# Who transposes the rows of experts 0 and 1: TensorE in place of VectorE

## The chip, the cores and the metric

The kernel runs on one core of a Trainium2 chip. Its engines are TensorE (PE: matrix products, with PEld for its weight loads), VectorE (DVE), ScalarE (ACT), GpSimd (POOL) and SyncE (SP), which here issues the DMA transfers. The metric is the device time of one execution in microseconds. Before the change three runs took 1133.36, 1134.56 and 1135.92 us, with a median of 1134.56.

## The reference

Three layers follow one another on 2304 tokens of width 512 (4 batches x 576 positions, 8 heads of 64):

```
scores = q k^T / 8 + decay (sums of log f), causal softmax, times v       -> x (2304 x 512)
h = x w_in (512 x 2048);  x = (h * sigmoid(1.702 h)) w_out (2048 x 512)
logits = x w_gate + log1p(exp(x w_noise)) * noise;  the two best of 8 experts, softmax of the two
out = sum over both of  weight * (max(x w1[e], 0) w2[e])                  (w1: 512 x 1024, w2: 1024 x 512)
```

The result is float32. The kernel gets that precision on TensorE by splitting each operand in a rounded part (hi) and a remainder (lo) and adding three products: hi x hi, lo x hi, hi x lo.

## The kernel before, in words

The order of all instructions is written at build time by a planner (class `Planner`, line 57). Every piece of work is a generator that yields operations with an engine and an estimated time, waits for events, or takes numbered tokens (a buffer). When several operations are ready on an engine, the one with the lowest priority number goes first. Each engine then runs its list in order, SyncE's list of transfers too; on the chip an instruction still waits until its inputs are there and its buffer is free.

The first expert layer (w_in, w_out) runs over 9 chunks of 256 tokens, in four passes over quarters of the hidden width. In its last pass each finished chunk is routed (`route`, line 1143): TensorE transposes the 2 x 4 blocks of the chunk (line 1159), ScalarE copies the rounded part (1162), VectorE subtracts the remainder (1163), then come the logits, some 25 small VectorE operations that find the two experts and the places, and four indirect writes by GpSimd (line 1264) that put each token's row, 512 values and 4 of metadata (`ROW` = 516), into the table `tab` at the place of its expert. Priority numbers of this layer start at 10000.

The second layer works on groups of table rows (`group`, line 1374). There are ten: group 0 and 1 hold the first 256 rows of experts 0 and 1 and are loaded early, when the sixth of nine chunks has been scattered; groups 2 and 3 hold their other 384 rows; groups 4 to 9 hold 640 rows each of experts 2 to 7. Group g has priority 20000 + 100 g; the transposes of its rows have 130 less, its weights 30 less. A group's rows are loaded by SyncE (line 1402), transposed (1435), copied by ScalarE (1438), subtracted by VectorE (1439); then for each of 8 blocks of the hidden width comes the first product h (line 1496), the copies of its parts (1479, 1480), and the second product ye (1549), whose result is scaled and added to the output by an indirect transfer (1536).

VectorE's transpose works on 32 x 32 squares only. So the rows are loaded with four transfers for each part, one for each 32 partitions, each row in four pieces of 128 values (512 bytes), such that the squares that VectorE transposes lie right:

```
for i in range(4):
    nc.sync.dma_start(t[32 * i:32 * i + 32, 4 * b0_:4 * b1_], bass.AP(
        tensor=tab.tensor, offset=tab.offset + (r0 + b0_ * 128) * ROW + i * part,
        ap=[[ROW, 32], [32 * ROW, 4 * (b1_ - b0_)], [1, part]]))
```

The columns of w_out are permuted on the host so that the features of a row come out in the order that this needs, and w1 is used as it is. The 4 values of metadata come with one more transfer for each group (line 1407).

Weights (`wprep`, line 348) are loaded in blocks of 256 KB into one of four staging buffers (`stok`, `NST` = 4), rounded by ScalarE (398), subtracted by VectorE or GpSimd (345, 346), and kept in 5 places for w1 and 6 for w2. The four staging buffers also serve the routing, which takes two of them for its transposed parts until the logits are done, and groups 0 and 1: each takes two, one for the rows as loaded (`xe`) and one for the rows as transposed (`xf`), and later one for each scaled output block. Groups 2 to 9 have buffers of their own.

Of the kernel before, what the change touches and what calls it, by code (L numbers as in the profile page):

```python
# [17 lines left out]
DRAM = bass.MemoryType.DRAM  # L18

TINY = 2.0 ** -15  # L20
CAP = 640
EARLY = 256
NEE = 2
ROW = 516
# [182 lines left out]
def dma(nbytes):  # L207
    return 0.05 + nbytes / RATE
# [7 lines left out]
def tile_attn_mlp_moe(ctx, tc, q, k, v, f, w_in, w_out, gates, noise, w1, w2, out):  # L216
# [52 lines left out]
    def c_(shape, name, dt=F32):  # L269
        return const.tile(shape, dt, name=name)  # L270
# [1098 lines left out]
    eids = [c_([128, NBE], f"eids{e}", I32) for e in EE]  # L1369
    ewab = [c_([128, 2, NBE], f"ewab{e}") for e in EE]  # L1370
    xftok = Tokens(range(2))
    emeta = [c_([128, NBE, ROW - DM], f"emeta{e}") for e in EE]

    def group(gi_):
        e, b0, b1 = groups[gi_]
        nb = b1 - b0
        N = nb * 128
        small = gi_ < len(EE)
        prio = 20000 + gi_ * 100
        if small:  # L1380
            yield scat[FLOOR]
            xs_, fs = yield from stages(2)
            t = stage(xs_, [128, 4 * nb, DM // 4], F32, "xe")
            xf = stage(fs, [128, nb, KD, 128], F32, "xf")
            ids, wab, mt = eids[gi_], ewab[gi_], emeta[gi_]
        else:
            yield m2_go
            xs_ = yield xetok
            xf = None
            t = M["x"].tile([128, 4 * nb, DM // 4], F32, name="xe", tag=f"xe{xs_}")  # L1390
            mt = M["x"].tile([128, nb, ROW - DM], F32, name="mt", tag=f"mt{gi_}")
            ids = M["x"].tile([128, nb], I32, name="ids", tag=f"ids{gi_}")
            wab = M["x"].tile([128, 2, nb], F32, name="wab", tag=f"wab{gi_}")
        r0 = e * RS + b0 * 128
        part = DM // 4
        parts = [(0, nb)] if gi_ <= 2 else [(0, 2), (2, nb)]
        lev = [event() for _ in parts]
        mev = event()

        def load(b0_, b1_):  # L1400
            for i in range(4):
                nc.sync.dma_start(t[32 * i:32 * i + 32, 4 * b0_:4 * b1_], bass.AP(
                    tensor=tab.tensor, offset=tab.offset + (r0 + b0_ * 128) * ROW + i * part,
                    ap=[[ROW, 32], [32 * ROW, 4 * (b1_ - b0_)], [1, part]]))

        def meta():
            nc.sync.dma_start(mt, tab[r0:r0 + N, DM:ROW].rearrange("(b p) c -> p b c", p=128))
        for (b0_, b1_), z in zip(parts, lev):
            yield ("go", one_op(("DMA", dma((b1_ - b0_) * 128 * DM * 4), lambda b0_=b0_, b1_=b1_: load(b0_, b1_), 4), z))
        yield ("go", one_op(("DMA", 0.4, meta), mev))  # L1410
        if small:
            for z in lev:
                yield z
            yield mev
            loads[0] -= 1
            if not loads[0]:
                yield ("set", early_ok)
            sl = yield ring
            x = xslot(sl)
            hi_, lo_ = x.hi, x.lo  # L1420
        else:
            sl = yield xttok
            hi_, lo_ = [M["x"].tile([128, KD, N], FR, name=f"xt{z}", tag=f"xt{z}{sl}") for z in "hl"]
        stt = nc.vector.scalar_tensor_tensor
        tev = [event() for _ in range(nb)]

        def xtr(b, z):
            yield z
            hi, lo = hi_[:, :, b * 128:(b + 1) * 128], lo_[:, :, b * 128:(b + 1) * 128]
            if small:  # L1430
                raw = xf[:, b]
            else:
                fi = yield xftok
                raw = M["x"].tile([128, KD, 128], F32, name="xf", tag=f"xf{fi}")
            yield ("DVE", dve(512), lambda: nc.vector.transpose(
                raw.rearrange("p k (j b) -> p j k b", b=32),
                t[:, 4 * b:4 * b + 4].rearrange("p j (k a) -> p j k a", a=32)))
            yield ("ACT", act(512, True), lambda: nc.scalar.copy(hi, raw))
            yield ("DVE", dve(512), lambda: nc.vector.tensor_tensor(lo, raw, hi.bitcast(F32), op=OP.subtract))
            if not small:  # L1440
                yield (xftok, fi)
            yield ("set", tev[b])
        for (b0_, b1_), z in zip(parts, lev):
            for b in range(b0_, b1_):
                yield ("go", xtr(b, z), prio - XTP)
        yield mev
        yield V(lambda: stt(wab[:, 0], mt[:, :, 3], float(NT), block[:, 0:nb], op0=OP.is_ge, op1=OP.mult))
        yield V(lambda: nc.vector.tensor_tensor(ids, mt[:, :, 3], wab[:, 0], op=OP.add))
        yield V(lambda: stt(wab[:, 0], mt[:, :, 2], float(e), mt[:, :, 0], op0=OP.is_equal, op1=OP.mult))
        yield V(lambda: stt(wab[:, 1], mt[:, :, 2], float(e), mt[:, :, 1], op0=OP.not_equal, op1=OP.mult))  # L1450
        yield V(lambda: nc.vector.tensor_tensor(wab[:, 0], wab[:, 0], wab[:, 1], op=OP.add))
        for z in tev:
            yield z
        yield (stok if small else xetok, xs_)
        if small:
            yield (stok, fs)

        if gi_:
            yield mm1_end[gi_ - 1]
        halves = [(0, N)] if N <= 512 else [(0, N // 2), (N // 2, N)]  # L1460
        H_ = []
        hev = [event() for _ in range(FB)]
        yield ("go", second(gi_, H_, hev, ids, wab, prio), prio - 5)
        for j in range(FB):
            wt = W2[gi_, "a", j]
            yield wt.ready
            if small:
                hs = yield gtok
                hh, hl = [gplace[hs].tile([128, N], FR, name=f"g{z}", tag=f"g{z}{hs}") for z in "hl"]
            else:  # L1470
                hs = yield htok
                hh, hl = [M["h"].tile([128, N], FR, name=f"h{z}", tag=f"h{z}{hs}") for z in "hl"]
            H_.append((hh, hl, hs))
            a0, a1 = [z.rearrange("p (k n) -> p k n", k=KD) for z in (wt.hi, wt.lo)]
            ops = [(a, z, kk) for a, z in ((a0, hi_), (a0, lo_), (a1, hi_)) for kk in range(KD)]
            ends = []

            def evac(ps, hh, hl, c0, c1, bi, end):
                yield ("ACT", act(c1 - c0), lambda: nc.scalar.activation(hh[:, c0:c1], ps, AF.Relu))  # L1479
                yield ("DVE", dve(c1 - c0), lambda: stt(  # L1480
                    hl[:, c0:c1], ps, 0.0, hh[:, c0:c1].bitcast(F32), op0=OP.max, op1=OP.subtract))
                yield (banks, bi)
                yield ("set", end)

            def both(ends, end):
                for z in ends:
                    yield z
                yield ("set", end)
            for c0, c1 in halves:
                bi = yield banks  # L1490
                ps = bank(bi, "h")[:, :c1 - c0]

                def part(i0, i1):
                    for i in range(i0, i1):
                        a, z, kk = ops[i]
                        nc.tensor.matmul(ps, a[:, kk], z[:, kk, c0:c1], start=(i == 0), stop=(i == len(ops) - 1))  # L1496
                yield ("PE", mm(c1 - c0, 6), lambda: part(0, 6))
                yield ("PE", mm(c1 - c0, 6), lambda: part(6, 12))
                end = event()
                ends.append(end)  # L1500
                yield ("go", evac(ps, hh, hl, c0, c1, bi, end), prio - 20)
            yield ("go", both(ends, hev[j]))
            yield from wt.used()
        if small:
            yield (ring, sl)
        else:
            yield (xttok, sl)
        yield ("set", mm1_end[gi_])
# [89 lines left out]
    with tc.If(most > 0), ExitStack() as octx:  # L1598
# [3 lines left out]
        for e in range(E):  # L1602
# [13 lines left out]
            with tc.For_i(0, nb) as i:  # L1616
# [10 lines left out]
                                               op0=OP.not_equal, op1=OP.mult)  # L1627
                nc.vector.tensor_tensor(wa, t1, t2, op=OP.add)
                nat = one.tile([128, KD, 4, 32], F32, name="nat")
                nc.vector.tensor_copy(nat, row[:, 0:DM].rearrange("p (i k a) -> p k i a", i=4, k=KD))  # L1630
                ps = psum.tile([128, KD, 128], F32, name="otr")
                for kk in range(KD):
                    nc.tensor.transpose(ps[:, kk], nat[:, kk].rearrange("p i a -> p (i a)"), identf)
# [19 lines left out]
def lay(I):  # L1653
# [16 lines left out]
    def words(w):  # L1670
# [6 lines left out]
    gates = gates.reshape(-1, 128, gates.shape[1]).transpose(1, 0, 2)  # L1677
    noise = I["moe2_noise"]
    noise = noise.reshape(-1, 128, noise.shape[1]).transpose(1, 0, 2)
    a = dict(q=q, k=k, v=v, f=I["f"], w_in=words(blocks(I["moe_w_in"])), w_out=words(I["moe_w_out"][:, order]), gates=gates,  # L1680
             noise=noise, w1=blocks(I["moe2_w1"]), w2=I["moe2_w2"])
    return {n: np.ascontiguousarray(x) for n, x in a.items()}


# [16 lines left out]
```

## Time and profile before

| | |
|---|---|
| median of three runs | 1134.56 us |
| profiled execution | 1138.96 us, span 1137.1 us, mean granted clock 0.989 |
| TensorE matmul | 1092.4 us busy, 96% of the span |
| VectorE / ScalarE / GpSimd | 716.3 / 516.8 / 248.1 us, 63% / 45% / 22% |
| DMA | 168.85 MB, 148 GB/s over the span |
| chain that ended last | PE 73%, DVE 9%, DMA 4%, issue 3% |

Times are from the span's start. Attention, with the first products of the first expert layer between its work, runs until 233 us; that layer ends at about 644 us, the second layer's last matmul at about 1118 us; the last output transfers and the closing test for overfull experts follow. "Granted clock" is the share of 2.4 GHz that TensorE was given: 1.00 or about 0.5 (1.2 GHz) in a short stretch.

### The profile page before, as it was taken

To read this page: it belongs to the slowest core of one execution; us is meant where nothing else is said; L and a number is where in the kernel's file an instruction comes from. 1 tells how busy PE (TensorE), PEld (TensorE's weight loads), DVE (VectorE), ACT (ScalarE), POOL (GpSimd) and SP (SyncE) were. 2 spreads that over 40 slices of the span, in tenths; PEclk is the share of its full clock that TensorE was granted. 3 is DMA by queue.
4 is the path that set the end of the run, shared out by engine and by line. 5 is a ranking of instruction groups with operands and counts; after the bars stand their busy time and mean duration, and the time that the engine had idled before them with its cause. 6 is when DMAs were issued, how large, how long until landed. Compare 5 with 4: busy or idle time off the path is not lost.

```text
span 1137.1 us, 18945 instructions
## 1 busy us (share of the span) xinstructions
PE 1092.4 (96%) x6836; PEld 960.6 (84%) x6836; DVE 716.3 (63%) x1783; ACT 516.8 (45%) x1234; POOL 248.1 (22%) x283
## 2 busy tenths in 40 slices
PE   9999989999999999999999998899999999999993
PEld 7778768898998998998999876789999999999992
DVE  7899988856688459446888887476353535353310
ACT  6688777745453334224333444355233334242311
POOL 2245423321012001001244340132030303030302
PEclk9999999999999999999999999999999999999997
DMA  7767666767869913000112478987353635252403
GB/s 228 235 224 245 190 216 200 183 182 185 279 169 313 378 38 105 10 1 10 39 75 79 146 231 215 219 211 187 98 127 115 131 117 116 88 113 85 103 1 50
DMA packets 111897, 168.85 MB, mean 148 GB/s; under 512 B 16752, under 2 KB 54384, under 8 KB 111792
## 3 DMA queue, kind: packets, MB, share of 16 engines
q1 hardware_dynamic: 103152, 147.53, 43.6%
q0 software_dynamic: 8640, 20.00, 8.5%
q8 instruction: 56, 0.92, 0.4%
q14 instruction: 49, 0.40, 0.1%
HBM read 118.16 MB, written 49.32 MB: 147 GB/s over the span
## 4 chain that ended last, share of the span: by engine, by line
PE 73%; DVE 9%; DMA 4%; issue 3%; ACT 2%; POOL 1%; SPq 0%; POOLq 0%; ACTq 0%; DVEq 0%
PE h L951 17%; PE h L1496 17%; PE ye L1549 16%; PE y L971 16%; PE O L745 3%; DMA wraw<-in_w 2%; DVE pt24l L457 1%; PE PT L699 1%; ACT e L591 1%; PE S L610 1%; DVE e L585 1%; DVE wbl L345 1%; DMA out<-yt,eids 1%; PE tr L1159 1%; POOL out L1536 1%
## 5 line engine op out<-in xcount | busy, mean ns | idle before, releaser
L1480 DVE SCALAR_TENSOR_TENSOR hl<-h,hh 128x320 fp32r<-128x320 f32 (+1 forms) x112 | 55.7, 498 | 187.3 <-ACT hh L1479 187.2
L1479 ACT ACTIVATE hh<-h 128x320 fp32r<-128x320 f32 (+1 forms) x112 | 49.8, 445 | 215.9 <-PE h L1496 215.7
L1536 POOL DMA_INDIRECT out<-yt,ids x36 | 61.0, 1693 | 281.6 <-ACT yt L1531 274.2
L1549 PE MATMUL ye<-wbh,hh 128*128 128x512 f32 x288 | 114.4, 397 | 1.0 <-ACT hh L1479 1.0
L1549 PE MATMUL ye<-wbh,hl 128*128 128x512 f32 x288 | 114.7, 398 | 0.1
L1549 PE MATMUL ye<-wbl,hh 128*128 128x512 f32 x288 | 114.5, 397 | 0.0
L971 PE MATMUL y<-wbh,gh 128*128 128x512 f32 x288 | 113.4, 394 | 0.6 <-DVE pt01l L457 0.3
L971 PE MATMUL y<-wbh,gl 128*128 128x512 f32 x288 | 112.9, 392 | 0.3 <-POOL gl L346 0.2
L971 PE MATMUL y<-wbl,gh 128*128 128x512 f32 x288 | 112.7, 391 | 0.0
L926 ACT ACTIVATE t<-h 128x256 f32<-128x256 f32 x144 | 55.3, 384 | 121.8 <-PE h L951 109.7
L591 ACT ACTIVATE e<-e,m 128x128 f32<-128x128 f32 (+2 forms) x144 | 83.1, 581 | 29.7 <-DVE m L585 29.1
L1496 PE MATMUL h<-xth,wah 128*128 128x320 f32 (+1 forms) x448 | 85.7, 313 | 3.2 <-ACT wah L398 3.2
L927 DVE SCALAR_TENSOR_TENSOR t<-t,h 128x256 f32<-128x256 f32 x144 | 60.2, 418 | 43.0 <-ACT t L926 37.0
L1496 PE MATMUL h<-xtl,wah 128*128 128x320 f32 (+1 forms) x448 | 87.0, 313 | 0.0
L1496 PE MATMUL h<-xth,wal 128*128 128x320 f32 (+1 forms) x448 | 85.7, 313 | 0.0
L346 POOL TENSOR_TENSOR gl<-t,gh 128x256 fp32r<-128x256 f32 x28 | 29.6, 1059 | 237.5 <-PE h L951 191.2
L1496 PEld LDWEIGHTS h<-xth,wah 128*128 128x128 f32 x448 | 73.2, 188 | 8.3 <-ACT wah L398 3.5
L929 ACT CAST gh<-t 128x256 fp32r<-128x256 f32 x125 | 50.7, 406 | 55.1 <-DVE t L927 55.0
L1496 PEld LDWEIGHTS h<-xtl,wah 128*128 128x128 f32 x448 | 72.3, 188 | 0.8
L1496 PEld LDWEIGHTS h<-xth,wal 128*128 128x128 f32 x448 | 71.6, 188 | 0.0
L345 DVE TENSOR_TENSOR gl<-t,gh 128x256 fp32r<-128x256 f32 x116 | 50.8, 439 | 29.0 <-ACT gh L929 26.9
L345 DVE TENSOR_TENSOR wbl<-wraw,wbh 128x512 fp32r<-128x512 f32 x76 | 57.1, 753 | 18.8 <-ACT wbh L398 17.9
(417 smaller groups left out, 2627.3 us busy)
## 6 DMA issues: line engine op xcount, KB each, us to landing
wraw<-in_w SPq DMA_DIRECT2D x160, 256.0 KB
tab<-padr SPq DMA_DIRECT2D x40, 258.0 KB
x<-xo SPq DMA_DIRECT2D x32, 288.0 KB
bb<-cneg SPq DMA_DIRECT2D x15, 576.0 KB
wraw<-in_w_in SPq DMA_DIRECT2D x16, 512.0 KB
wraw<-in_w_out SPq DMA_DIRECT2D x16, 512.0 KB
out<-padr SPq DMA_DIRECT2D x23, 256.0 KB
xa<-x SPq DMA_DIRECT2D x22, 256.0 KB
```

Of the source, the lines that this page charges most:

```text
L345: return ways(kind, ("DVE", dve(n), lambda: nc.vector.tensor_tensor(dst, a, b, op=OP.subtract)), ("POOL", pool2(n), lambda: nc.gpsimd.tens ...
L591: yield ("ACT", act(n, True, extra=2), lambda: nc.scalar.activation(dst, dst, AF.Exp, bias=m[:, x:x + 1], scale=-1.0, accum_out=sa[:, shar ...
L926: yield ("ACT", act(CH), lambda: nc.scalar.activation(t, h, AF.Tanh, scale=0.851))
L927: yield ("DVE", dve(CH), lambda: nc.vector.scalar_tensor_tensor(t, t, 1.0, h, op0=OP.add, op1=OP.mult))
L929: yield ways("gh", ("ACT", act(CH, True), lambda: nc.scalar.copy(gh, t)), ("POOL", pool1(CH), lambda: nc.gpsimd.tensor_tensor(gh, t, onec. ...
L951: nc.tensor.matmul(h, a[:, kk], z[:, kk], start=(i == 0), stop=(i == len(ops) - 1))
L971: nc.tensor.matmul(y, a[:, t * 128:(t + 1) * 128], b, start=(fl == 0 and n == 0), stop=(fl == FPQ - 1 and n == 2))
L1479: yield ("ACT", act(c1 - c0), lambda: nc.scalar.activation(hh[:, c0:c1], ps, AF.Relu))
L1480: yield ("DVE", dve(c1 - c0), lambda: stt(hl[:, c0:c1], ps, 0.0, hh[:, c0:c1].bitcast(F32), op0=OP.max, op1=OP.subtract))
L1496: nc.tensor.matmul(ps, a[:, kk], z[:, kk, c0:c1], start=(i == 0), stop=(i == len(ops) - 1))
L1536: st = nc.gpsimd.indirect_dma_start(out=out, out_offset=bass.IndirectOffsetOnAxis(ap=ids[:, b:b + 1], axis=0), in_=yt, in_offset=None, com ...
L1549: nc.tensor.matmul(ye[b][0], a[:, b * 128:(b + 1) * 128], w, start=(j == 0 and n == 0), stop=(j == FB - 1 and n == 2))
```

## The change

`PEX` = 2 names the experts, 0 and 1, whose groups (0 to 3) are now "whole". Their rows are loaded as they lie in the table, 2064 bytes a row with the metadata, one transfer for each block of 128 rows. TensorE transposes each block with four 128 x 128 transposes into a PSUM bank, from which ScalarE copies and VectorE subtracts. The rows of w1 of these two experts are permuted on the host in the same way as the columns of w_out. The buffers for transposed rows and for early metadata are gone for groups 0 and 1, so each takes one staging buffer. Groups 4 to 9 keep VectorE's transpose; the planner's price for their loads is doubled, that for their metadata raised from 0.4 to 1.0. The branch for overfull experts, which doesn't run work here, follows the layout.

```diff
+PEX = 2
-    emeta = [c_([128, NBE, ROW - DM], f"emeta{e}") for e in EE]
+        whole = e < PEX
         if small:
             yield scat[FLOOR]
-            xs_, fs = yield from stages(2)
-            t = stage(xs_, [128, 4 * nb, DM // 4], F32, "xe")
-            xf = stage(fs, [128, nb, KD, 128], F32, "xf")
-            ids, wab, mt = eids[gi_], ewab[gi_], emeta[gi_]
+            xs_ = yield stok
+            t = stage(xs_, [128, nb, ROW], F32, "xe")
+            ids, wab = eids[gi_], ewab[gi_]
...
-        parts = [(0, nb)] if gi_ <= 2 else [(0, 2), (2, nb)]
+        parts = [(b, b + 1) for b in range(nb)] if whole else [(0, 2), (2, nb)]
         def load(b0_, b1_):
+            if whole:
+                nc.sync.dma_start(t[:, b0_], tab[r0 + b0_ * 128:r0 + b1_ * 128, :])
+                return
...
-            yield ("go", one_op(("DMA", dma((b1_ - b0_) * 128 * DM * 4), lambda b0_=b0_, b1_=b1_: load(b0_, b1_), 4), z))
-        yield ("go", one_op(("DMA", 0.4, meta), mev))
+            yield ("go", one_op(
+                ("DMA", dma((b1_ - b0_) * 128 * DM * (4 if whole else 8)), lambda b0_=b0_, b1_=b1_: load(b0_, b1_),
+                 1 if whole else 4), z))
+        if whole:
+            mt = t[:, :, DM:ROW]
+        else:
+            yield ("go", one_op(("DMA", 1.0, meta), mev))
...
-            if small:
-                raw = xf[:, b]
+            if whole:
+                bi = yield banks
+                raw = bank(bi, "tr").rearrange("p (k n) -> p k n", k=KD)
+
+                def go():
+                    for kk in range(KD):
+                        nc.tensor.transpose(raw[:, kk], t[:, b, kk * 128:(kk + 1) * 128], identf)
+                yield ("PE", TR * KD, go)
             else:
...
-            yield ("ACT", act(512, True), lambda: nc.scalar.copy(hi, raw))
+            yield ("ACT", act(512, not whole), lambda: nc.scalar.copy(hi, raw))
             yield ("DVE", dve(512), lambda: nc.vector.tensor_tensor(lo, raw, hi.bitcast(F32), op=OP.subtract))
-            if not small:
-                yield (xftok, fi)
+            yield (banks, bi) if whole else (xftok, fi)
...
+    w1 = np.concatenate([I["moe2_w1"][:PEX][:, order], I["moe2_w1"][PEX:]])
-             noise=noise, w1=blocks(I["moe2_w1"]), w2=I["moe2_w2"])
+             noise=noise, w1=blocks(w1), w2=I["moe2_w2"])
```

## Rows read from the trace of the kernel before

**Rows 1.** Stretches: busy PE, PEld, DVE, ACT, POOL; PE clock, DMA share, GB/s.

```profile
600.00:640.00 40.00, 39.99 (x274) 36.18 (x273) 34.26 (x160) 14.00 (x36) 13.94 (x25) 1.00 0.29 94
640.00:670.00 30.00, 27.07 (x175) 22.46 (x174) 25.91 (x118) 13.86 (x31) 10.00 (x16) 1.00 0.55 176
...
680.00:700.00 20.00, 16.55 (x86) 12.84 (x85) 11.64 (x23) 8.02 (x17) 2.64 (x3) 0.91 0.93 221
700.00:710.00 10.00, 9.60 (x50) 7.64 (x50) 9.14 (x21) 6.01 (x12) 0.00 (x0) 1.00 0.67 196
710.00:730.00 20.00, 16.83 (x77) 14.75 (x76) 8.04 (x19) 6.72 (x14) 3.27 (x3) 0.91 1.04 242
...
750.00:770.00 20.00, 18.84 (x89) 15.39 (x88) 15.03 (x24) 9.35 (x18) 6.10 (x6) 1.00 1.01 237
770.00:1113.00 343.00, 343.00 (x1908) 310.35 (x1906) 145.98 (x273) 115.66 (x236) 56.82 (x63) 1.00 0.42 104
```

**Rows 2.** The same table for two short stretches behind gaps of PE.

```profile
688.70:691.90 3.20, 3.20 (x9) 2.53 (x9) 1.91 (x6) 0.62 (x1) 0.00 (x0) 0.51 1.18 259
722.60:726.00 3.40, 3.40 (x10) 2.64 (x9) 1.99 (x3) 1.57 (x3) 0.00 (x0) 0.51 1.18 245
```

**Rows 3.** Waits of PE, 620 to 800: us in total, times, longest.

```profile
PE h L1496 <- ACT wah L398: 3.5, 2, 3.2
PE ye L1549 <- ACT gh L1479: 3.4, 3, 2.4
PE l L1189 <- DVE lgs L1182: 1.3, 1, 1.3
```

**Rows 4.** Timeline of SyncE's queue, 625 to 700: start, us, line, transfer, count.

```profile
630.33 1.82 SPq L1402 DMA_DIRECT2D xe<-tab  x4
...
641.95 45.19 SPq L365 DMA_DIRECT2D wraw<-in_w  x23
```

**Rows 5.** Chain that ended last, 600 to 800: start, us, what.

```profile
604.86 1.43 PE h L951 x12
606.41 0.93 PE tr L1159 x8
...
710.62 7.21 DMA out<-yt,eids
...
720.51 0.63 ACT wah L398
...
769.50 4.18 PE ye L1549 x18
```

**Rows 6.** Waits of SyncE's queue, 600 to 800: us in total, times, longest.

```profile
SPq L365 <- DMA out<-yt,eids: 12.1, 4, 6.2
...
SPq L365 <- DVE ewab L1447: 4.9, 1, 4.9
```

**Rows 7.** Timelines of DVE and PE: start, us, engine, line, operation, [idle].

```profile
632.89 0.68 DVE L1323 SCALAR_TENSOR_TENSOR pay<-y,yacc 128x512 f32<-128x512 f32 x1
...
643.82 1.03 PE L1159 MATMUL tr<-identf,pay 128*128 128x128 f32 x8
...
693.47 1.31 DVE L1435 STREAM_TRANSPOSE xf<-xe 128x512 f32<-128x512 f32 x2 [2.04 <-DMA xe<-tab]
```

**Rows 8.** Four lines: ns of one (min/median/max), first and last start.

```profile
L1159 PE MATMUL tr<-identf,pay x72: 270/273/308, 538.0 to 652.9; 128*128 128x128 f32 x72
...
L1162 ACT CAST yth<-tr x18: 585/590/595, 538.6 to 653.3; 128x512 fp32r<-128x512 f32 x18
...
L1163 DVE TENSOR_TENSOR ytl<-tr,yth x18: 673/678/692, 539.3 to 655.1; 128x512 fp32r<-128x512 f32 x18
...
L1435 DVE STREAM_TRANSPOSE xf<-xe x40: 664/704/716, 636.4 to 1009.4; 128x512 f32<-128x512 f32 x40
```

**Rows 9.** Stretches with row loads alone (first) and weight loads alone (second).

```profile
631.00:637.00 6.00, 6.00 (x50) 5.72 (x49) 5.58 (x29) 1.79 (x5) 0.00 (x0) 1.00 0.76 179
912.00:916.00 4.00, 4.00 (x23) 3.52 (x22) 3.34 (x6) 2.18 (x5) 0.00 (x0) 1.00 0.54 185
```

More of the change, by code (lines that the diff above doesn't have):

```diff
@@ L1388, in group @@
             xs_ = yield xetok
-            xf = None
-            t = M["x"].tile([128, 4 * nb, DM // 4], F32, name="xe", tag=f"xe{xs_}")
-            mt = M["x"].tile([128, nb, ROW - DM], F32, name="mt", tag=f"mt{gi_}")
+            t = M["x"].tile([128, NB * ROW], F32, name="xe", tag=f"xe{xs_}")
+            if whole:
+                t = t[:, 0:nb * ROW].rearrange("p (b c) -> p b c", c=ROW)
+            else:
+                t = t[:, 0:nb * DM].rearrange("p (j c) -> p j c", c=DM // 4)
+                mt = M["x"].tile([128, nb, ROW - DM], F32, name="mt", tag=f"mt{gi_}")
             ids = M["x"].tile([128, nb], I32, name="ids", tag=f"ids{gi_}")
@@ L1408, in group @@
         for (b0_, b1_), z in zip(parts, lev):
-            yield ("go", one_op(("DMA", dma((b1_ - b0_) * 128 * DM * 4), lambda b0_=b0_, b1_=b1_: load(b0_, b1_), 4), z))
-        yield ("go", one_op(("DMA", 0.4, meta), mev))
+            yield ("go", one_op(
[3 more added lines that the diff above has]
+            mt = t[:, :, DM:ROW]
+        else:
+            yield ("go", one_op(("DMA", 1.0, meta), mev))
         if small:
@@ L1413, in group @@
                 yield z
-            yield mev
             loads[0] -= 1
@@ L1429, in xtr @@
             hi, lo = hi_[:, :, b * 128:(b + 1) * 128], lo_[:, :, b * 128:(b + 1) * 128]
-            if small:
-                raw = xf[:, b]
+            if whole:
+                bi = yield banks
[4 more added lines that the diff above has]
+                yield ("PE", TR * KD, go)
             else:
@@ L1434, in xtr @@
                 raw = M["x"].tile([128, KD, 128], F32, name="xf", tag=f"xf{fi}")
-            yield ("DVE", dve(512), lambda: nc.vector.transpose(
-                raw.rearrange("p k (j b) -> p j k b", b=32),
-                t[:, 4 * b:4 * b + 4].rearrange("p j (k a) -> p j k a", a=32)))
-            yield ("ACT", act(512, True), lambda: nc.scalar.copy(hi, raw))
+                yield ("DVE", dve(512), lambda: nc.vector.transpose(
+                    raw.rearrange("p k (j b) -> p j k b", b=32),
+                    t[:, 4 * b:4 * b + 4].rearrange("p j (k a) -> p j k a", a=32)))
+            yield ("ACT", act(512, not whole), lambda: nc.scalar.copy(hi, raw))
             yield ("DVE", dve(512), lambda: nc.vector.tensor_tensor(lo, raw, hi.bitcast(F32), op=OP.subtract))
-            if not small:
-                yield (xftok, fi)
+            yield (banks, bi) if whole else (xftok, fi)
             yield ("set", tev[b])
@@ L1445, in group @@
                 yield ("go", xtr(b, z), prio - XTP)
-        yield mev
+        if whole:
+            for z in lev:
+                yield z
+        else:
+            yield mev
         yield V(lambda: stt(wab[:, 0], mt[:, :, 3], float(NT), block[:, 0:nb], op0=OP.is_ge, op1=OP.mult))
@@ L1454, in group @@
         yield (stok if small else xetok, xs_)
-        if small:
-            yield (stok, fs)
         if gi_:
@@ L1629, in tile_attn_mlp_moe @@
                 nat = one.tile([128, KD, 4, 32], F32, name="nat")
-                nc.vector.tensor_copy(nat, row[:, 0:DM].rearrange("p (i k a) -> p k i a", i=4, k=KD))
+                if e < PEX:
+                    nc.vector.tensor_copy(nat, row[:, 0:DM].rearrange("p (k i a) -> p k i a", i=4, k=KD))
+                else:
+                    nc.vector.tensor_copy(nat, row[:, 0:DM].rearrange("p (i k a) -> p k i a", i=4, k=KD))
                 ps = psum.tile([128, KD, 128], F32, name="otr")
```

## The prediction

> **What bounds the kernel now.** First the page's busy shares and slices: TensorE (PE) is busy for 96% of the span, so what counts is where it isn't. I read PE's idle time by stage from the table of stretches [rows 1]. From 600 to 640 (end of the first expert layer) PE is busy 39.99 of 40 us. From 770 to 1113 it is busy 343.00 of 343: experts 2 to 7 run without a gap, and nothing outside PE can gain or lose there. Between them lie the routing of the last token chunks and groups 0 to 3, the rows of experts 0 and 1, which are the only ones that the change moves to PE. There PE is idle 2.93 us (640 to 670), 3.45 (680 to 700), 0.40 (700 to 710), 3.17 (710 to 730) and 1.16 (750 to 770). After two of these gaps its granted clock is 0.51 for 3.2 and 3.4 us [rows 2], the 1.2 GHz level: 0.49 x 3.2 = 1.6 and 0.49 x 3.4 = 1.7 us more. So 680 to 700 loses 5.0 us, 710 to 730 loses 4.9.
>
> The waits of PE [rows 3] name the causes: weights not yet rounded (3.5 us on ACT wah), first-product copies queued behind such weights on ScalarE (3.4 on ACT gh), VectorE late with logits (1.3 on DVE lgs). So this stretch is bound by weight supply, and the queue that feeds it says why: the first weight load of the second layer is issued at 641.95, and 23 take 45.19 us, 1.96 us each [rows 4]. PE uses one weight block per 1.43 us (first product, 12 matmuls of 256 columns; the row is the first layer's, of the same shape) or 6 x 4.18 / 18 = 1.39 us (second) [rows 5]. Supply starts late and is slower than demand.
>
> It starts late because of the four staging buffers. Groups 0 and 1 take two each (rows, transposed rows) and hold all four from about 630 until VectorE has transposed and split; the load waited 4.9 us for VectorE's group work [rows 6]. The routing of the last chunk but one wants two as well: its payload is finished at 633.57, but its transposes run only at 643.82 [rows 7]. So both last routings, some 25 small VectorE operations each, fall into 643 to 672, where VectorE is busy 25.91 of 30 us [rows 1] and holds up both logits and weights.
>
> **The change part by part.** *PE transposes.* 10 blocks (2+2+3+3) of 4, 40 in all. The routing's transposes have the same form: 8 take 0.93 us in the chain [rows 5], 0.1163 us each, so +4.65 us of PE work. Their listed duration is 273 ns each [rows 8], but they overlap.
> The Trainium skill (TensorE: Matmul & The Clock Gate, Part 4: PE-mode transpose) gives some 275 ns for a transpose inside a kernel: the duration agrees with the row, the pace doesn't; by 275 ns each the term would be 11.0 instead of 4.65, and the sum below +3.3. The same section says that transposes don't raise the clock as matmuls do, which speaks against the change; around the 8 at 606 the granted clock is 1.00 [rows 1], so the sum goes without it and both stand among the rivals.
>
> *First rows.* Groups 0 and 1 were transposed by VectorE before PE needed them. On PE their transposes have a planner number near 20000 against some 10000 of the first layer, so they come behind its last product at 643.8. Group 0's first matmul then waits for two blocks: transposes 0.47, two ScalarE copies of 0.59, one VectorE subtraction of 0.68 [rows 8], 2.33 us; all 16 transposes of both groups cover 1.86. I take 0.8 with hand-overs; bounds 0 (routing work fills it) and 2.3 (group 1's don't come in between). For groups 2 and 3 this latency lies beside the previous group's matmuls.
>
> *VectorE.* 10 transposes of 0.704 us go [rows 8], 7.0 us, 2.8 of them before 643. Copies and subtractions stay; from PSUM the routing's take 0.590 and 0.678, like the group's. This is part of the recovery below.
>
> *Staging.* Each small group holds one buffer instead of two. So the last routing but one can begin at about 634 instead of 643.8, and leaves 643 to 672 to the last one. Its two buffers come back some 4 us later and serve weight loads from about 638, 4 us earlier than 641.95. Recovered from 640 to 670: 2.3 of 2.93 (bounds 0 and 2.93; what is left is the last routing's own). From 680 to 700: 4 us more supply is two to three weights of 1.43, that is 2.8 to 4.3 us of PE's work, and VectorE frees buffers sooner: 4.0 of 5.0 (bounds 0 and 5.0).
>
> *Loads.* Before, each load is 4 transfers in pieces of 512 B, issued in 1.82 us [rows 4], plus one for the metadata; groups 0 to 3 have 24 transfers, after 10. While rows alone were moving, the engines carried 179 GB/s at a share of 0.76, 236 per full share; weights, 2 KB a piece as the whole rows will be, 185 at 0.54, 343 [rows 9]. A block of 262 KB costs 1.11 us before and, if it moves like weights, 0.76: for the six blocks of groups 2 and 3, 2.1 us of transfer between 687 and 705, inside the recovery above and below (bounds 0 and 2.1).
> The Trainium skill (DMA: Bandwidth & Descriptors, Specifications) calls 512 B enough for line rate; by it this 2.1 would be 0. The rows of this case disagree, 236 against 343; it would take at most 2.1 us off the recovery.
>
> *The loss at 710 to 730.* The scatter of group 1's output takes 7.21 us and keeps a staging buffer; weight loads wait 6.2 us behind it, and ScalarE gets the weight at 720.51 [rows 5, 6]. The change doesn't touch that chain. A lead of one or two weights (2.1 us each in group 2: 9 of the 18 matmuls above) shortens its effect: 2.2 of 4.9 (bounds 0 and 4.9).
>
> *The other six experts.* Their instructions stay; only the planner's price for their loads doubles and that for metadata rises, which moves places in queues. PE has no gap behind 770 to lose or to fill, and DMA is at 0.42 [rows 1]: 0, and if that cover fails, the gaps of 750 to 770 show the size, 1.2 us.
>
> **Sum.** +4.65 + 0.8 - 2.3 - 4.0 - 2.2 = -3.05 us. The profiled execution took 1138.96 us (span 1137.1 and 1.9 around it), 4.4 above the median of 1134.56 and above the highest run; on its own time the sum gives 1135.9, on the median 1131.5, which I predict.
>
> **The rivals.**
> *Supply gains too little (same).* If the two freed buffers go to the routing first and weights get only the two left, two weights of lead are all: 2.3 + 2.8 = 5.1 recovered against 5.45, +0.35, 1134.9. For it: three loads of the layer are out early and the next need slots that the first layer frees only from about 634. Against it: VectorE's 7.0 us.
> *PE waits for rows (slower).* Place: the transposes of groups 2 and 3. Their planner number (20070, 20170) lies before the first matmuls of groups 1 and 2 (20100, 20200), so they are put into PE's queue in front of running work as soon as the plan thinks the rows there. Before, VectorE waited 2.04 us at 693.47 for group 2's rows [rows 7] and PE went on; after, PE itself would stand, and the weights' matmuls behind it. Price: 2.0 for one such wait and 1.6 of low clock behind it [rows 2], with only 2.3 + 2.2 recovered since the gap stays: 4.65 + 0.8 + 3.6 - 4.5 = +4.55, 1139.1. It decides where waits ahead of transposes and unrecovered loss exceed 5.3 us together (-3.05 turns to +2.3). Against it: each block has its own transfer, so the first arrives before three are complete.
> *All of it recovered (faster).* With 2.93 + 5.0 + 4.9 = 12.8 against 5.45, -7.4, 1127.2. Against it: the scatter's chain stays.
> *Dear transposes (slower, or same).* At their listed 273 ns the 40 cost 10.9, the sum is +3.2, 1137.8; against it, the pace of 8 in 0.93. If the clock falls behind group 0's 16 transposes and the wait after them, 1.6 more [rows 2], -1.45, 1133.1; against it, the clock of 1.00 around the routing's 8, but these lie between matmuls. The section cited above speaks for both.
> *It isn't what it says:* if the planner puts the routing behind the groups all the same, nothing of 640 to 670 comes back: -0.75, 1133.8.
>
> **How the numbers follow.** A change of this kernel is told from none at about 0.2%, 2.3 us. Forecast 0.45 (-2.3 to -6), all recovered 0.07, same 0.24 (supply 0.12, low clock 0.07, nothing of the routing 0.05), slower 0.24 (rows waited for 0.22, 273 ns each 0.02). Faster is 0.45 + 0.07 = 0.52. The likeliest one's own range is 1128.5 to 1132.3. With the unknown bounds the total runs from -8.2 (12.8 recovered, no first gap) to +10.6 (nothing recovered, 4.65 + 2.3 + 3.6); the range goes down to that end, 1126.5, since much of this was bounded by gaps that are there to be filled, and up to the slower rival's 1139; beyond that several bounds would have to meet.
>
> **What would show it.** Right: the routing's transposes of the last chunk but one near 635; the first weight load of the second layer before 640 with a smaller spacing than 1.96 us; 40 transposes on PE near 0.116 us each; PE idle in 640 to 700 under 2.5 us; VectorE's stream transposes down from 40 to 30; experts 2 to 7 as before. Wrong: waits of PE on row loads, a low clock after group 0's transposes, or gaps behind 770.

## The result, and the profile after

The changed kernel takes 1122.87 us (median of six runs, 1121.22 to 1127.59) against 1135.11 (six runs, 1133.36 to 1138.18): ratio 0.9904, 95% interval 0.9883 to 0.9925: 12 us faster by the medians, 11 by the ratio. Forecast were 1131.5 us and at best 1126.5. The sign was right; the size, and the range, were not.

The profiled execution took 1121.46 us; its span, 1119.7, is 17.4 us shorter than the one of before. Not all of that is the change's: the first routing transposes start at 532.30 instead of 537.95, and up to there both programs do the same work (from other addresses). Over all kernels below this start lies anywhere from 531.8 to 539.2. So I measure from it, to the last output transfer of each group (the 2nd, 4th, 7th, 10th and then every fifth of the 40 indirect output transfers in GpSimd's timeline):

| us from the first routing transposes to the end of | group 0 | 1 | 2 | 3 | 4 | 9 |
|---|---|---|---|---|---|---|
| before | 141.8 | 174.5 | 212.7 | 247.5 | 309.0 | 583.5 |
| after | 143.0 | 170.8 | 206.4 | 238.3 | 299.5 | 572.0 |

That makes -11.5 us: +1.2 in the first row, -10.4 over groups 1 to 3, and -2.3 between group 3 and group 9, where the forecast had nothing.

Stretches of the kernel after (columns as in [rows 1]):

```profile
600.00:640.00 40.00, 39.81 (x278) 35.29 (x277) 33.38 (x159) 14.90 (x38) 16.69 (x31) 1.00 0.35 120
640.00:670.00 30.00, 28.20 (x190) 24.25 (x189) 25.62 (x103) 15.12 (x33) 6.96 (x11) 1.00 0.59 178
670.00:680.00 10.00, 9.55 (x60) 8.23 (x59) 5.93 (x12) 4.64 (x9) 5.98 (x10) 1.00 0.92 256
680.00:700.00 20.00, 17.71 (x113) 15.50 (x114) 13.18 (x28) 10.86 (x22) 0.00 (x0) 1.00 0.76 245
700.00:710.00 10.00, 10.00 (x57) 9.34 (x57) 6.37 (x15) 4.71 (x9) 3.46 (x4) 1.00 0.92 178
710.00:730.00 20.00, 20.00 (x102) 17.98 (x101) 10.49 (x17) 8.15 (x16) 0.00 (x0) 1.00 0.94 247
...
750.00:770.00 20.00, 20.00 (x108) 18.45 (x107) 13.25 (x24) 10.55 (x21) 4.23 (x6) 1.00 0.79 200
```

PE's idle time of 11.3 us between 630 and 770 is down to 4.7, the clock stays at 1.00, and the whole gap of 710 to 730 is gone, not half of it. Waits of PE, 600 to 1100, in the form of [rows 3]:

```profile
PE h L1513 <- ACT wah L399: 1.9, 1, 1.9
PE h L1513 <- DVE cumc L1247: 0.8, 1, 0.8
PE h L1513 <- DVE xrl L1455: 0.7, 1, 0.7
PE ye L1566 <- ACT gh L1496: 0.5, 1, 0.5
PE tr L1446 <- DMA xe<-tab: 0.4, 1, 0.4
...
```

SyncE's queue and PE around the start of the second layer, to be held against [rows 4, 7]:

```profile
625.27 1.75 SPq L1405 DMA_DIRECT2D xe<-tab  x4
633.01 48.43 SPq L366 DMA_DIRECT2D wraw<-in_w  x24
681.49 0.42 SPq L1405 DMA_DIRECT2D xe<-tab  x1
```

```profile
628.95 1.07 PE L1160 MATMUL tr<-identf,pay 128*128 128x128 f32 x8
...
641.62 1.47 PE L1446 MATMUL tr<-identf,xe 128*128 128x128 f32 x12
643.30 0.63 PE L1446 MATMUL tr<-identf,xe 128*128 128x128 f32 x4
...
644.71 0.71 PE L1513 MATMUL h<-xrh,wah 128*128 128x256 f32 x4 [0.78 <-DVE cumc L1247]
...
646.10 0.74 PE L1513 MATMUL h<-xrl,wah 128*128 128x256 f32 x4 [0.68 <-DVE xrl L1455]
```

Of the signs that the forecast named, these are there: routing early (628.95, before 643.82), weights from 633.01 instead of 641.95, 30 stream transposes instead of 40, no wait for rows beyond 0.4. These are not: the weight loads are no closer together (48.43 / 24 = 2.02 us, before 1.96), PE is idle for 4.5 us from 640 to 700 where under 2.5 was forecast, and experts 2 to 7 run faster than before. Whether the signs that came are the cause is another question; the experiments answer it.

**A loss that the idle column does not show.** Between one `ye` matmul and the next lie 0.23 us, but each is listed with 0.39 to 0.40 (rows under "experts 2 to 7" below). A listed matmul covers 0.16 us of its successor, so of every wait some 0.16 us count as busy. The Trainium skill (Perfetto Trace Analysis, Identifying the Most-Contended Engine) says that matmul busy share does not show how close TensorE is to its roofline, because pipelined instructions look smaller in the trace. In this trace they are listed longer than they are apart (0.39 against 0.23 us), and that hides waits. Taking start-to-start times less the undisturbed spacing of each shape, from 630 to the end of group 3, I get a loss of 22.8 us before (idle time and half clock together: 14.6) and 8.0 after (4.7); other choices of the undisturbed spacing give 21 to 23 and 8 to 10. So some 14.8 were recovered, of which the column shows 9.9; less 4.65 for the transposes this is -10.2, against -9.2 from the table.

### The profile page after: what moved, and what is told of

Same layout as the page of the kernel before. It is cut to its first block, busy times and chain, and to the rows that moved or that the text cites. A ratio compares the mean times of both kernels' runs of the same rounds, so it can differ in the third digit from the quotient of the medians.

```text
span 1119.7 us, 18985 instructions
## 1 busy us (share of the span) xinstructions
PE 1083.4 (97%) x6876; PEld 956.8 (85%) x6876; DVE 711.1 (64%) x1777; ACT 516.5 (46%) x1233; POOL 242.4 (22%) x280
## 4 chain that ended last, share of the span: by engine, by line
PE 79%; DVE 7%; ACT 3%; DMA 2%; issue 2%; POOL 1%; POOLq 0%; SPq 0%; ACTq 0%; DVEq 0%
PE h L1513 19%; PE ye L1566 18%; PE h L952 17%; PE y L972 17%; PE O L746 3%; PE PT L700 1%; PE S L611 1%; ACT e L592 1%; DVE pt24l L458 1%; DVE e L586 1%; POOL out L1553 1%; PE tr L1160 1%; DMA out<-yt,eids 1%; DVE kl L346 0%; DMA wraw<-in_w 0%
## 5 line engine op out<-in xcount | busy, mean ns | idle before, releaser
L972 PEld LDWEIGHTS y<-wbh,gl 128*128 128x128 f32 x288 | 54.0, 188 | 16.0 <-POOL gl L347 1.8
```

Source lines behind the costliest of these rows:

```text
L972: nc.tensor.matmul(y, a[:, t * 128:(t + 1) * 128], b, start=(fl == 0 and n == 0), stop=(fl == FPQ - 1 and n == 2))
```

## The experiments

All ratios are to the kernel before on the same chip, with 95% intervals. Two columns come from each kernel's one profiled execution: us from the first routing transposes to the end of group 3, and from there to the end of group 9. Kernels that should be alike up to group 3 (after, f1, g3) read 238.0 to 240.4 in the first column, so a difference of some 2 us there tells nothing.

| kernel | ratio | to group 3 | 3 to 9 |
|---|---|---|---|
| before | 1 | 247.5 | 336.0 |
| after | 0.9904 [0.9883, 0.9925] | 238.3 | 333.7 |
| e1 second buffers held | 0.9977 [0.9954, 1.0000] | 243.3 | 338.1 |
| e2 before, staging alone | 1.0025 [1.0001, 1.0048] | 252.8 | 336.0 |
| e3 before, prices alone | 1.0007 [0.9986, 1.0027] | 247.7 | 334.1 |
| e4 after, old prices | 0.9927 [0.9898, 0.9956] | 246.4 | 333.5 |
| e5 whole rows, VectorE | 0.9899 [0.9869, 0.9930] | 237.3 | 333.6 |
| e6 pieces, TensorE | 0.9958 [0.9942, 0.9974] | 242.4 | 336.5 |
| e7 transposes twice | 0.9925 [0.9898, 0.9953] | 242.3 | 333.6 |
| e8 before, staging and prices | 1.0044 [1.0019, 1.0068] | 249.2 | 337.9 |
| f1 after, all shifted 64 bytes | 0.9895 [0.9865, 0.9924] | 240.4 | 334.0 |
| f2 before, all shifted 64 bytes | 1.0017 [0.9998, 1.0035] | 247.6 | 336.0 |
| f3 experts 2 and 3 too | 0.9953 [0.9935, 0.9971] | 241.3 | 338.9 |
| f4 groups 0 and 1 alone | 1.0027 [1.0000, 1.0055] | 249.6 | 336.1 |
| g1 before, hidden shifted | 0.9980 [0.9960, 1.0001] | 245.7 | 333.5 |
| g2 after, hidden shifted | 0.9918 [0.9887, 0.9949] | 240.4 | 336.3 |
| g3 after, first layer shifted | 0.9889 [0.9857, 0.9920] | 238.0 | 333.8 |
| g4 groups 2 and 3 alone | 0.9934 [0.9914, 0.9954] | 238.6 | 335.3 |

### Is it the staging?

e1, the changed kernel with the second buffer taken and left unused:

```diff
-            xs_ = yield stok
+            xs_, fs = yield from stages(2)
...
         yield (stok if small else xetok, xs_)
+        if small:
+            yield (stok, fs)
```

> The changed kernel, but groups 0 and 1 hold a second, unused staging buffer until their rows are transposed, as before. Theory S (staging: the freed buffers let the last routing but one and the weight loads start earlier, and that is most of the 12 us): the routing's transposes fall behind the first layer's end again, the first weight load near 641 to 645, and at least 6 of the 12 us are lost: 1129 to 1137 us. Rival P (the planner's new price for row loads gives a better order) and rival T (loads in whole rows and 7 us less VectorE work): 1121 to 1126 us, since both are still in.

e2, the kernel before with the transposed rows of groups 0 and 1 in the dead tiles of an earlier chunk, one staging buffer each; e3, the new planner prices alone; e8, both:

```diff
...
-            xs_, fs = yield from stages(2)
+            yield turns[NQ - 1, rest[0]]
+            xs_ = yield stok
...
-            xf = stage(fs, [128, nb, KD, 128], F32, "xf")
+            xf = late.tile([128, nb, KD, 128], F32, name=f"xf{e}", tag=f"x{"hl"[e]}{rest[0]}")
...
```

> The kernel before with one edit: the transposed rows of groups 0 and 1 lie in the dead buffer of an earlier chunk instead of a staging buffer, so each group holds one staging buffer. VectorE transposes everything, loads and prices as before. Theory S: most of the gain without TensorE's 4.65 us of transposes: 1119 to 1127 us, routing's transposes near 630 to 636, first weight load before 640. Rivals P and T: 1131 to 1136 us.

> The kernel before with the planner's prices of the changed one for groups 4 to 9 alone (row loads doubled, metadata 1.0 instead of 0.4); nothing else differs than the order in which the planner puts instructions. Theory S and rival T: 1133 to 1137 us, no change. Rival P: at least 4 us faster, 1131 us or less, with the loss of TensorE behind 700 us gone.

> The kernel before with both the dead buffer in place of the second staging buffer and the new prices for groups 4 to 9; rows in 512 B pieces and VectorE's transposes as before. If these two together are the change's gain (rival P with S): 1119 to 1126 us. If whole rows or TensorE's transposes are needed (L or T): 1132 to 1140 us, near the staging edit alone.

e1 seemed to settle it for staging: by the ratios some 8 of 11 us gone, the routing's transposes at 643.02, the first weight load at 643.22. But its trace doesn't put the loss there. TensorE starts group 4 235.8 us after the first routing transposes, in the kernel after 234.7. Most of the loss comes then, in group 4, where GpSimd has a weight's remainder queued behind output transfers:

```profile
778.07 1.78 POOL L1555 DMA_INDIRECT out<-yt,ids  x1 [0.27 <-ACT xth L1454]
779.29 1.85 POOL L347 TENSOR_TENSOR wal<-wraw,wah 128x512 fp32r<-128x512 f32 x1
```

```profile
781.19 1.44 PE L1515 MATMUL h<-xth,wal 128*128 128x320 f32 x4 [3.72 <-POOL wal L347]
```

After these 3.72 us the granted clock is 0.50 until 785 and 0.79 until 789, some 2.8 us more. (The table's 243.3 goes by group 3's last output transfer, which is late too.) So e1 shows the price of another order of instructions; for the second buffers themselves it shows 1.1 us up to group 4, which is within the noise.

e2 speaks against staging too: its routing runs at 629.81 and its first weight load at 633.86, as early as in the kernel after, and it is slower than before: what it wins up to group 0 (141.0) it gives back in groups 1 to 3. Prices add nothing without the rest (e3, e8). e4 takes them back from the changed kernel:

```diff
-                ("DMA", dma((b1_ - b0_) * 128 * DM * (4 if whole else 8)), lambda ...
+                ("DMA", dma((b1_ - b0_) * 128 * DM * 4), lambda ...
-            yield ("go", one_op(("DMA", 1.0, meta), mev))
+            yield ("go", one_op(("DMA", 0.4, meta), mev))
```

> The changed kernel with the planner's old prices (row loads of groups 4 to 9 at half the price, metadata 0.4). Theory S and rival T: 1121 to 1126 us. Rival P: 1127 us or more, with waits of TensorE behind 700 us back.

By the ratios the prices are worth 0.0023, some 2.6 us, with intervals that overlap; the one profile lost more than that (its execution is the slowest of nine).

### Is it the engine that transposes, or the loads?

e5 keeps the whole rows and gives the transposes of groups 0 to 3 back to VectorE (features come out in another order than the weights have). e6 keeps TensorE's transposes and loads the rows in pieces of 512 bytes again (same remark):

```diff
 e5
...
-                        nc.tensor.transpose(raw[:, kk], t[:, b, kk * 128:(kk + 1) * 128], identf)
+                yield ("DVE", dve(512), lambda: nc.vector.transpose(
+                    raw.rearrange("p k (j b) -> p j k b", b=32),
+                    t[:, b, 0:DM].rearrange("p (j k a) -> p j k a", j=4, a=32)))
...
 e6
...
-                nc.sync.dma_start(t[:, b0_], tab[r0 + b0_ * 128:r0 + b1_ * 128, :])
-                return
+                if b0_:
+                    return
+                meta()
+                b1_ = nb
...
```

> The changed kernel in everything (whole-row loads, one staging buffer, new prices) except that VectorE transposes the blocks of groups 0 to 3 again, into a dead buffer. Its squares lie wrong with whole rows, so the numbers of experts 0 and 1 are wrong; the amount of work is that of before. So far staging alone gained nothing and undoing it lost nearly all, so something else must go with it. Theory L (the loads in whole rows, 2 KB a piece instead of 512 B, go with it): 1116 to 1124 us, since TensorE's 4.65 us also go. Theory T (VectorE's time goes with it): 1130 us or more.

> The changed kernel in everything (TensorE transposes, one staging buffer, prices and order) except that the rows of groups 0 to 3 come in pieces of 512 B again, four transfers a group and one for metadata, into the same places in time. The blocks are put together wrong, so the numbers of experts 0 and 1 are wrong; the amount of work is the same. Theory L: 1130 us or more. Theory T: 1121 to 1126 us.

The engine makes no difference (e5, 0.9899): on TensorE the transposes win back about what they cost there. The loads do. e8 and e5 both have one staging buffer for each small group, the new prices and VectorE's transposes; e8 loads in pieces and takes 249.2 us to the end of group 3, e5 loads whole rows and takes 237.3. With TensorE's transposes e6 loses 4.1 us there and, by the ratios, more than half of the gain; the 2.8 us that it loses behind group 3 go with its addresses (`d` is 64 in all six places; see experts 2 to 7 below). Its PE at 684 shows one wait that the kernel after has too and one that it has not:

```profile
684.02 0.74 PE L1512 MATMUL h<-xrh,wah 128*128 128x256 f32 x4 [1.96 <-ACT wah L399]
689.38 1.09 PE L1445 MATMUL tr<-identf,xe 128*128 128x128 f32 x4 [3.66 <-DMA xe<-tab]
```

That is the forecast's slower rival, PE standing in front of rows, but only with rows in pieces: e6's four transfers bring the two or three blocks of a group together, so that its first block is there only with the last, and PE waits 3.66 us where single whole blocks make it wait 0.4. Whether the pieces of 512 bytes or the missing split by blocks costs this, no run separates.

f4 and g4 split the change by groups:

```diff
 f4
-        whole = e < PEX
+        whole = small
 g4
...
-        whole = e < PEX
+        whole = gi_ in (2, 3)
...
```

> The changed kernel with whole rows and TensorE's transposes for groups 0 and 1 alone; groups 2 and 3 are loaded in pieces and transposed by VectorE as before (their weights' rows stay permuted, so the products of these groups are not the reference's). If the gain comes from the small groups' loads and staging: 40 - 24 = 16 transposes remain, 2.8 us less of TensorE's work, so 1120 to 1123. If the whole-row loads of groups 2 and 3 carry half of it: loss from group 1 to group 3 rises by 3 to 6 us, 1124 to 1127. With the pieces experiment at +8 us as the upper end.

> The changed kernel with whole rows and TensorE's transposes for groups 2 and 3 alone; groups 0 and 1 are loaded in pieces into two staging buffers each and transposed by VectorE as before (w1 stays permuted, so their products are not the reference's). Theory S (staging and early supply carry most): like the kernel that held the second buffers, 1132 to 1134, ratio 0.998. Theory L (the load of groups 2 and 3 in 512-byte pieces is what costs, wherever the staging stands): 1125 to 1127, ratio 0.991 to 0.993, with 16 transposes less (1.9 us) than the changed kernel.

f4 has the early start (routing at 628.47, first weight load at 632.53) and no gain, 249.6. It isn't quite the kernel before in groups 2 and 3: group 2's rows come in eight transfers, before in four, and the planner prices the loads of both groups at double. g4 is the cleaner half. It has the loads and buffers of before for groups 0 and 1, and the late start:

```profile
645.01 1.03 PE L1160 MATMUL tr<-identf,pay 128*128 128x128 f32 x8
```

```profile
631.49 1.82 SPq L1410 DMA_DIRECT2D xe<-tab  x4
...
643.10 45.42 SPq L366 DMA_DIRECT2D wraw<-in_w  x23
688.57 0.43 SPq L1407 DMA_DIRECT2D xe<-tab  x1
```

and still reaches the end of group 3 after 238.6 us, as the kernel after does (with 16 transposes, 1.9 us, less on TensorE). The gain up to there comes from groups 2 and 3, not from staging. What went wrong in f4, where they stay in pieces with VectorE, can be read in its trace. The chain that leads to PE's stalls at 707 and 708:

```profile
698.78 5.28 DMA out<-yt,eids
...
704.19 0.06 DVE yt L1546
...
704.86 1.29 DVE xf L1451 x2
706.15 0.57 DVE wbl L346
706.73 1.07 DVE xtl L1455 x2
...
707.85 0.56 DVE hl L1497
...
708.45 2.99 PE ye L1566 x7
```

VectorE waits with group 1's scaled output (`yt`) for a staging buffer that the output transfer before it holds for 5.28 us. Behind it in VectorE's queue are the transposes of the next group's rows. ScalarE in turn has put the copies of these rows in front of the hidden block that PE needs:

```profile
705.59 1.21 ACT L1454 CAST xth<-xf 128x512 fp32r<-128x512 f32 x2 [4.26 <-DVE xf L1451]
706.71 0.49 ACT L1496 ACTIVATE hh<-h 128x384 fp32r<-128x384 f32 x1
```

```profile
707.25 0.50 PE L1566 MATMUL ye<-wbh,hh 128*128 128x512 f32 x1 [2.78 <-ACT hh L1496]
```

So one output transfer stops VectorE, VectorE stops ScalarE, ScalarE stops PE. This chain explains f4, not the gain: e5 has VectorE's transposes too and loses nothing, and in the kernel before ScalarE waited for rows no longer than in the kernel after, 2.7 us in all (longest 1.1) against 3.7 for `tr` (longest 1.3). What is shorter after, between 675 and 770, are ScalarE's waits for weight loads, 10.6 us instead of 27.3. The first two lines are before's, the last three after's:

```profile
ACT wah L398 <- DMA wraw<-in_w: 13.7, 7, 8.3
ACT wbh L398 <- DMA wraw<-in_w: 13.6, 6, 4.7
```

```profile
ACT wah L399 <- DMA wraw<-in_w: 6.8, 7, 2.1
ACT wbh L399 <- DMA wraw<-in_w: 3.8, 5, 1.4
...
ACT xth L1454 <- PE tr L1446: 3.7, 4, 1.3
```

SyncE's queue fits this. It needs 6 x 0.42 us to issue the rows of groups 2 and 3, where before it spent some 1.9 on each of three sets of four transfers, and in 680 to 700 the engines move 245 GB/s at a share of 0.76, 322 per full share, against 221 / 0.93 = 238 before. So weights come earlier: by 180 us after the first routing transposes it has issued 36 weight loads before (counted from 641.95), 41 after (from 633.01), 40 in e5, 41 in g4, 38 in e6. TensorE's wait for a weight of 3.2 us, at 183 us on this scale in the kernel before, stands at the same place in f2, g1, e2 and e8 (2.9 to 3.4 us), and in no kernel that loads groups 2 and 3 in whole rows. (e3, e6 and f4 load them in pieces and wait elsewhere.) That the earlier weights end this wait is the likeliest reading; no run changes them alone.

### What do the transposes cost?

e7 runs each transpose twice (the second writes the same values); f3 extends the change to experts 2 and 3:

```diff
 e7
-                    for kk in range(KD):
+                    for kk in list(range(KD)) * 2:
 f3
-PEX = 2
+PEX = 4
```

> The changed kernel with each of TensorE's 40 transposes of rows issued twice into the same place. It prices them in their place: if they lie on the path in full, +4.65 us, 1127 to 1128 us; if gaps cover them, 1123 to 1124 us; by their listed 273 ns each, +10.9 us, 1134 us.

> The change carried on to experts 2 and 3 (groups 4 and 5, 640 rows each): 10 more blocks, 40 more transposes on TensorE. By the doubled transposes (40 more at 0.116 us, +4.65 forecast, +4.7 measured) 1127 to 1128, unless whole-row loads win there too, which they can't where TensorE has no gap behind group 3 (loss 0.7 and 0.6 us a group): at best 1126. Rival: group 4's loads collide with the weights of groups 2 and 3, and whole rows relieve them by 1 to 3 us: 1124 to 1125.

e7 is 4.7 us above the changed kernel's median (by the ratios 0.0021, 2.4 us), and 4.0 in the column up to group 3. That excludes the listed 274 ns, 10.9 us, and agrees with the forecast's 0.116 without fixing it. The trace does: e7's 80 transposes of rows take 9.2 us from start to start, 0.115 each. f3 shows where the change stops paying: behind group 3 PE has no gap, and whole rows win nothing there; 338.9 instead of 333.7. By the ratios it is 5.6 us slower than the changed kernel, more than either of its theories said.

### What changed in experts 2 to 7?

In the profiles groups 4 to 8 follow each other every 56.1 us before and every 55.65 after. All of it lies in the second product: 15 `ye` matmuls take 3.49 to 3.50 us from the first to the next block's `h`, after the change 3.42 to 3.45. f1 and f2 shift all tiles behind the constants by 64 bytes:

```diff
+    pad = [c_([128, NBE, ROW - DM], f"pad{e}") for e in EE]
+    for z in pad:
+        nc.gpsimd.memset(z, 0.0)
```

> The changed kernel with two unused constant tiles of 64 bytes a partition in all put back where the early metadata lay, so that every later tile lies 64 bytes further. The six runs of other experiments fall in two kinds: with these tiles groups 4 to 8 follow at 56.1 us, without them at 55.65. Theory A (the place of the tiles in memory sets TensorE's pace): 56.1 us a group here too, 5.5 groups x 0.45 = 2.5 us more, 1125 to 1126. Theory O (the order of instructions or the loads set it): 55.65 and the changed kernel's time, 1122.9. Instructions and their order are those of the changed kernel but for two memsets.

> The kernel before with two more unused constant tiles behind the early metadata, so that every later tile lies 128 instead of 64 bytes beyond its place in the changed kernel. Theory A (place in memory, in steps of 128 bytes): 55.65 us a group, some 2.5 us faster than before, about 1132. Theory O (order of instructions or loads): 56.1 and no change.

Theory A falls: nothing moves. But the addresses of the tiles sort the blocks: with d = (address of `hh` - address of `wb`) modulo 256, mean us of a block over eight kernels (before, after, e5, e6, f1 to f4), 7 to 8 blocks in each of six weight places:

| d | 0 | 192 | 64 | 128 |
|---|---|---|---|---|
| us a block | 3.42 to 3.43 | 3.45 | 3.49 to 3.50 | 3.49 to 3.50 |

A few blocks with a wait in them are left out. g4, with all six places at 192, has 3.47 to 3.48.

The change moved d from 128 to 0 (four places) and 192 (two), because four of the six weight places lie 64 bytes lower (the early metadata in front of them, 64 bytes of constants, is gone), and `hh` lies 64 bytes higher (the row buffers in front hold the metadata now and are larger). g1 and g2 shift `hh` and `hl` alone; g3 does the same for the first layer's activations, whose d the change had made worse (64 instead of 0 in three of four pairs):

```diff
 g1, g2
+    nc.gpsimd.memset(M["h"].tile([128, 32], F32, name="padh", tag="padh"), 0.0)
 g3
+    nc.gpsimd.memset(gpool.tile([128, 48], F32, name="padg", tag="padg"), 0.0)
+    nc.gpsimd.memset(xpool.tile([128, 16], F32, name="padx", tag="padx"), 0.0)
```

> The kernel before with 128 unused bytes a partition in front of the activations hh and hl of experts 2 to 7, nothing else: their distance to the weights goes from 128 to 0 modulo 256 in all six places. Theory D (the distance sets the pace): a block of the second product 3.42 instead of 3.49 us, a group 8 x 0.07 = 0.6 less, 55.5 instead of 56.1; over about 5.8 groups 3.3 us faster, ratio 0.997. Theory O (something else of the change): 56.1 a group and no change.

> The changed kernel with the same 128 bytes: the distance goes from 0 (four places) and 192 (two) to 128 and 64. Theory D: 3.49 to 3.50 us a block and 56.1 us a group again, 2.5 us slower than the changed kernel: ratio to before 0.9925 instead of 0.9904. Theory O: 55.65 a group, and the changed kernel's ratio.

> The changed kernel with 192 unused bytes in front of the first layer's activations (gh, gl; four of five places) and 64 behind them, so that what lies further on keeps its place modulo 256. In the changed kernel the distance of gh to the weights became 64 for 608 of 813 pairs (before: 0), and their spacing 0.2325 us instead of 0.2275 to 0.229. Theory D: back to 0.228, some 500 x 0.004 = 2 us less in the first layer, before 644 us, if its waits leave it: ratio 0.988 to 0.989, a version better than both. Rival: the first layer has waits that take it up: 0.9904 and no difference.

One block each, first `ye` and the next `h`, of the kernel before, of g1, of the kernel after and of g2:

```profile
850.24 0.39 PE L1549 MATMUL ye<-wbh,hh 128*128 128x512 f32 x1
850.47 0.39 PE L1549 MATMUL ye<-wbl,hh 128*128 128x512 f32 x1
...
853.73 0.75 PE L1496 MATMUL h<-xth,wah 128*128 128x320 f32 x4
```

```profile
858.88 0.39 PE L1549 MATMUL ye<-wbh,hh 128*128 128x512 f32 x1
...
862.30 0.74 PE L1496 MATMUL h<-xth,wah 128*128 128x320 f32 x4
```

```profile
856.00 0.40 PE L1566 MATMUL ye<-wbh,hh 128*128 128x512 f32 x1
...
859.44 0.76 PE L1513 MATMUL h<-xth,wah 128*128 128x320 f32 x4
```

```profile
858.83 0.39 PE L1566 MATMUL ye<-wbh,hh 128*128 128x512 f32 x1
...
862.32 0.74 PE L1513 MATMUL h<-xth,wah 128*128 128x320 f32 x4
```

3.49 before and 3.42 in g1, 3.44 after and 3.49 in g2: the distance sets the pace, both ways, and the column "3 to 9" moves by -2.5 and +2.6. The total times agree in direction (0.9980 and 0.9918 against 0.9904), but their intervals are as wide as the effect. g3 has the lowest whole-kernel ratio, 0.9889, with the spacing of `y` back from about 0.2325 to 0.231; against the changed kernel's 0.9904 that is not told apart, so I claim no version better than both.

## Why the prediction was off, by its own steps

- *PE transposes, +4.65*: right (e7).
- *First rows, +0.8*: 0.78 and 0.68 us of waiting at 644.71 and 646.10, 1.5, inside its bounds of 0 and 2.3. The granted clock stays 1.00, so the low-clock rival did not occur.
- *Staging, 640 to 670, 2.3 of 2.93 recovered*: of the 1.80 us of idle time left, 1.46 are the first rows, so about 2.6; as forecast. But it is not worth time by itself: e2 and f4 have the early start and are no faster, g4 lacks it and has the gain, and in e1, which lacks it too, TensorE starts group 4 only 1.1 us later.
- *680 to 700, 4.0 of 5.0*: 2.29 idle are left, so 2.7; and not by the four microseconds of earlier supply that the step named.
- *The loss at 710 to 730, "the change doesn't touch that chain", 2.2 of 4.9*: this step failed. All 4.9 went, and the 0.40 and 1.16 of 700 to 710 and 750 to 770 with it: 6.5 instead of 2.2. The lead was about five weights (41 against 36 loads issued by 180 us), not one or two; that it ended this loss is likely and not isolated.
- *Loads, at most 2.1, "inside the recovery"*: this step failed worst as a cause. I priced the bytes and not the order: six single transfers take less of SyncE's queue than twelve parts, and rows arrive block by block. Up to group 3 pieces cost 4.1 us with TensorE's transposes (e6 against after) and 11.9 with VectorE's (e8 against e5), some 0.5 us of each by the addresses. How this splits between the size of the pieces, the split by blocks and the queue stays open.
- *The other six experts, 0*: failed, -2.3, by tile addresses (g1, g2); the forecast looked for gaps, and this is pace.
- *The way of sizing*: all bounds were read from the idle column. It showed 14.6 us where 22.8 were lost, so even "all recovered" (12.8, 1127.2) was too small. That the sign came out right owes less to the forecast's cause, the staging, than to the loads that it had counted as part of the recovery.

In sum: 8.5 recovered was forecast; 9.9 show in the column with the first rows already taken off, 4.9 more are hidden under listed durations, 2.3 lie behind group 3. The forecast's -3.05 and these corrections (9.9 - 7.7, 4.9, 2.3) make -12.45 against -11.5 from the table; the 1 us between is within what the choice of the undisturbed spacing leaves open.

## What to carry to other kernels

Size a loss on a pipelined engine from start-to-start times, not from the idle column, and bound a recovery by that. When one change moves an operation and also changes how its input is loaded, test the two apart: here the loads carried the gain, and the moved transposes won back about what they cost. And when a change drops or adds a small tile, compare the addresses of the later operands before giving the gain to the algorithm.

## What the hardware showed that I had not expected

TensorE's spacing for the same 512-column matmul depends on where its two operands lie relative to each other: 3.42 to 3.43 us for 15 of them at a distance of 0 bytes modulo 256, 3.45 to 3.48 at 192, 3.49 to 3.50 at 64 or 128, up to 2%, shown by moving one operand in two kernels. Shifting both together did nothing. In the first layer the distance alone is not the whole account: `y` matmuls follow at 0.229 us before, where all are at 0, and at 0.2305 and 0.2334 at 0 and 64 after. The 256-column `h`, whose operands are the other way round, follow at 0.120 at 0 and 0.115 to 0.117 at 192; those I did not move alone. Which part of the read path is behind it, no run here shows.
